# Block mask spread by copies, beta2 as an extra column, and a reordered first load in a sparse-attention and ResMLP kernel

## The chip, the cores and the metric

The kernel runs on one core of a Trainium2 chip. The metric is the device time of one execution in microseconds, and the figure quoted is the median of several runs. Engines are named as the profile names them: PE is TensorE's matmul stream and PEld its weight loads, DVE is VectorE, ACT is ScalarE, POOL is GpSimd, and SP is SyncE, which here issues DMAs only.

## The reference, cut to what matters

Two stages follow one another. The first is block-sparse attention over 4 batches of 8 heads, 768 positions, head size 64. A block of 32 keys is visible to a block of 32 queries if it is a neighbour, if either is the first or the last block, or if it is one of three sampled blocks of that query block.

```python
scores = scale * np.matmul(q, k.transpose(0, 1, 3, 2))
...
for qb in range(n_blocks):
    for kb in sampled_blocks[qb]:
        mask[qb * block:(qb + 1) * block, kb * block:(kb + 1) * block] = True
scores = np.where(mask, scores, -1000000000.0)
...
return np.matmul(attn, v).astype(np.float32)
```

The mask is the same for all heads and batches. The second stage takes the attention output, with the heads side by side, as x of 4 x 768 x 512:

```python
a1 = alpha1 * x + beta1
tok = np.einsum('ts,bsd->btd', w_tok, a1)
u = x + lam * tok
a2 = alpha2 * u + beta2
ch = np.maximum(a2 @ w_ch1, 0.0) @ w_ch2
return (u + lam * ch).astype(np.float32)
```

w_ch1 is 512 x 2048 and w_ch2 is 2048 x 512. Because beta2 is added before w_ch1, beta2 @ w_ch1 is a vector of 2048 numbers that is the same for every row. The kernel uses it as the bias of the ReLU.

## The kernel before, in words

**Tiling.** Work goes in 16 head pairs (four to a batch). Each pair has 9 units (lines 1014 to 1094). A unit is the transposed scores of one 128 x 1024 piece: matmuls into a PSUM tile `sps` of 1024 columns (`emit_qk_full`, L906, or `emit_qk_rows`, L925), one exponential on ACT into an fp16 tile `eT` (L935), and eight matmuls of 65 columns each that multiply `eT` by V and a column of ones (L961). Two `sps` tiles exist, and four one-bank tiles `gb` of 512 columns serve everything else. After the fifth and the ninth unit, DVE divides by the sum (L977, L980) and writes `x_sb`.

**Two ways to mask.** For pairs 0 to 4 (T0 = 5) the mask is part of the score matmul: 24 more contraction rows (the slice MB, partitions 64 to 87) hold, on the key side, an indicator of the key's block and, on the query side, 0 or -400. For pairs 5 to 15 the scores are made with 64 rows alone, two heads' halves of the array at a time, and DVE multiplies `eT` by a stored 0/1 mask `msk` of 128 x 2 x 2560 fp16 (L942, 99 times). The stored mask is built once (`mask_ops`, lines 697 to 745): six pairs of matmuls of 24 rows and 384 columns into `sps` (L707), six exponentials of 128 x 768 on ACT (L728), and one DVE copy of its first 256 columns to its end (L742). It is built from the indicator rows of pair 4's tile, and each `mult` depends on it.

**Preparing a pair.** Pairs 0 to 4 are transposed on PE (L418) and copied by DVE or ACT. From pair 5 on, SP issues DMA transposes of q (L812, two of them) and k (L835), and then two DMAs (`swap`, L855) that copy the first 384 query columns of one partition half to the other half, so that both row halves of the array have what they read. The matmuls of such a pair wait for all of these.

**The ResMLP.** After a pair, DVE makes `a1p` (L1130, L1141), PE mixes tokens (L1179), DVE adds (L1203) and scales to bf16 `ub` (L1217). `ub` is transposed to `uT`: by PE for batch 0, by SP's DMA transposes (L1289) for the others. When four pairs are done, the channel mixer runs in two halves of 384 rows for each batch. Each half has 16 groups of four matmuls of 384 columns into a `gb` bank (`ch1`, L1321), each followed by a ReLU with bias on DVE (L1351) or ACT (L1343), and then twelve groups of four matmuls of 512 columns (`ch2`, L1383). DVE adds the result (L1405) and SP stores it. The half numbered kk = 0 is the first of batch 0.

**The bias.** DVE casts beta2 to `be2b` (L652). Four groups of 16 one-column matmuls (L662) multiply it with w_ch1, and four DVE copies (L673) move four columns at a time to `b1t`, which the ReLUs read.

**The start.** SP issues `sampi` (the sampled blocks, L350), then the two halves of pair 0's q (L352, L354), then three small indicator loads (L356). ACT's queue issues pair 0's k (L351, L353). DVE makes a 24 x 24 block table `mbb` from `sampi` (L400, L406). PE multiplies it (L423), and DVE (L435) and ACT (L432) turn that into the mask rows. PE transposes the first k and then q (L418 by way of `transposes`), ACT and DVE copy them (L447), and the first score matmul follows. `keep_warm` matmuls (L385) fill gaps. In program order DVE's L400 and L406 stand ahead of the cast of q (L413), and PE's L423 stands ahead of both transposes.

**What sets the order.** All later work is given to a planner (`Plan`, lines 102 to 264). Every operation has a cost, a due time and dependencies; the planner simulates the engines, picks the ready operation that is due first, and thereby writes each engine's program order, which is then pinned. An operation offered to both DVE and ACT (`both`) goes to whichever is free first. Loads, DMA transposes and other DMAs have assumed durations (`queued`, `beside`). A list SEEDS shifts due times of early operations by random amounts. Costs and due times thus decide order only; they are not times of the chip.

Of the kernel before, what the change touches and what calls it, by code (L numbers as in the profile page):

```python
# [24 lines left out]
S = 768  # L25
# [21 lines left out]
T0 = 5  # L47
FINE = 3
SEEDS = [2000008, 2000011, 2000019, 2000022, 2000031, 2000062, 2000071, 2000092, 2000133, 2000145, 2000148, 2000158, 2000173, 2000177, 2000195, 2000260, 2000269, 2000429, 2000572, 2000889, 2001074, 2001979, 2002135]
# [52 lines left out]
class Plan:  # L102
# [3 lines left out]
    def __init__(self, pools, free):  # L106
        self.pools = {k: list(range(n)) for k, n in pools.items()}
        self.free = dict(free)
        self.ops = []
        self.users = {}  # L110
        self.slot = {}
        self.held = {}
        self.reader = {}
        self.shifted = False
        self.exps = 0
        self.dma = 6500.0
        self.ring = []
        self.occ = None
        self.loads = []
        self.hw = 0.0  # L120
        self.segs = []
# [146 lines left out]
def kernel(  # L268
# [51 lines left out]
    be2b = pp.tile([P, 4], BF, name="be2b", tag="be2b")  # L320
# [13 lines left out]
    uT = many(3, [P, 4, S], BF, "uT")  # L334
# [14 lines left out]
    k2f = wk.tile([P, 2, NT * D], FP, name="k2f", tag="hts", bufs=2)  # L349
    nc.sync.dma_start(sampi[MB, :], sampled_blocks.bitcast(I32))  # L350
    nc.scalar.dma_start(k2f[:, 0, :], pair_ap(k, 0, 0)[:, 0, :])  # L351
    nc.sync.dma_start(q2f[:, 0, :], pair_ap(q, 0, 0)[:, 0, :])  # L352
# [96 lines left out]
    for t in vext:  # L449
# [5 lines left out]
        dict(PE=5600, ACT=5600, DVE=5750, POOL=3700, SP=4000),  # L455
# [8 lines left out]
    def sl(key):  # L464
        return pl.slot[key][1]
# [91 lines left out]
    def bc_load(nm, t, src, due):  # L557
        def emit(op):
            nc.gpsimd.dma_start(t[:], src.unsqueeze(0).to_broadcast([P, DM]))

        BC[nm] = load(("bc", nm), 640, due, emit)
# [23 lines left out]
    LD[("v", 0)] = landed(("v", 0), 7200)  # L585
# [36 lines left out]
    for g in range(4):  # L622
# [29 lines left out]
        lambda op: nc.vector.tensor_copy(out=be2b[:], in_=be2T[:]),  # L652
# [3 lines left out]
    for g in range(4):  # L656
        key = ("mmb", g)

        def e_mm(op, g=g, key=key):
            for f in range(4):  # L660
                for dk in range(4):
                    nc.tensor.matmul(  # L662
                        bank(key)[:, f : f + 1],
                        w1b[:, dk, ts(4 * g + f, P)],
                        be2b[:, dk : dk + 1],
                        start=(dk == 0),
                        stop=(dk == 3),
                    )

        mm = pl.pe(("be2m", g), 420, 37 + 2.5 * g, e_mm, deps=[W1[g], be2c], need=[(key, GB)])  # L670

        def e_b(op, g=g, key=key):
            nc.vector.tensor_copy(out=b1t[:, ts(g, 4)], in_=bank(key)[:, 0:4])  # L673

        B1T.append(pl.dve(("b1t", g), 165, 36.5 + g, e_b, deps=[mm], uses=[key]))
# [20 lines left out]

    def mask_ops():
        for g in range(3):
            for r in range(2):
                key = ("sps", "m", g, r)  # L700
                due = 9 * T0 - 10 + 2 * g + r

                def e_mm(op, g=g, r=r, key=key):
                    i = sl(("qk", T0 - 1))
                    for w in range(2):
                        o = ORD[r][3 * w]
                        nc.tensor.matmul(  # L707
                            spsT[sl(key)][:, w * 512 : w * 512 + HS],
                            kx2[i][MB, 0, ts(2 * g + r, P)],
                            qx2[i][MB, 0, :].rearrange("p (o t) -> p o t", o=NT)[  # L710
                                :, o : NT : 2, :
                            ],
                            start=True,
                            stop=True,
                        )

                mm = pl.pe(
                    ("mskm", g, r),
                    520,
                    due,  # L720
                    e_mm,
                    deps=PREP[T0 - 1],
                    need=[(key, [("sps", 0)])],
                    uses=[("qk", T0 - 1)],
                )

                def e_x(op, g=g, r=r, key=key):
                    nc.scalar.activation(  # L728
                        msk[:, r, g * S : (g + 1) * S].rearrange("p (w c) -> p w c", w=2),
                        spsT[sl(key)][:].rearrange("p (w c) -> p w c", w=2)[:, :, 0:HS],  # L730
                        AF.Exp,
                        bias=0.0,
                        scale=SCALE,
                    )

                MASK.append(pl.act(("mskx", g, r), act(768), due, e_x, deps=[mm], uses=[key]))
        MASK.append(
            pl.dve(
                ("mskc",),
                dve(512, 4),  # L740
                9 * T0 - 3,
                lambda op: nc.vector.tensor_copy(out=msk[:, :, HF:MW], in_=msk[:, :, 0:256]),  # L742
                deps=MASK[0:2],
            )
        )
# [60 lines left out]
    def prep_rows(pi):  # L806
# [3 lines left out]
        def e_q(op, h):  # L810
# [5 lines left out]
            [("SP", 1250, beside(480, 1250))],  # L816
# [8 lines left out]
            [("SP", 1250, beside(480, 1250))],  # L825
# [7 lines left out]
        def e_k(op):  # L833
# [8 lines left out]
            [("SP", 1250, beside(960, 1250))],  # L842
# [7 lines left out]
        for r in range(2):  # L850

            def e_s(op, r=r):
                i = sl(key)
                lo, hi = slice(r * D, (r + 1) * D), slice((1 - r) * D, (2 - r) * D)
                nc.sync.dma_start(qx2[i][lo, :, HS:S], qx2[i][hi, :, 0:HS])  # L855

            res.append(
                pl.add(
                    ("swap", pi, r),
                    [("SP", 450, beside(380, 450, 40))],  # L860
                    9 * pi - 100,
                    e_s,
                    deps=[t0, t1],
                    uses=[key],
                )
            )
# [3 lines left out]
    for i in range(2):  # L870
# [5 lines left out]
            deps=[landed(("f", i), 5400 - 300 * i)],  # L876
# [140 lines left out]
    while i < NI:  # L1017
# [22 lines left out]
        occ = 437 if pi < T0 else 640  # L1040
# [11 lines left out]
        for j, key in zip(batch, keys):  # L1052
# [23 lines left out]
            for a in unit_heads(uj):  # L1076
# [5 lines left out]
                    30,  # L1082
# [13 lines left out]
    for pi in range(NP):  # L1096
# [188 lines left out]
        else:  # L1285
            for v2 in range(2):

                def e_ud(op, uk=uk, b=b, n=n - 1 + v2, v2=v2):
# [8 lines left out]
                        [("SP", 1250, beside(960, 1250))],  # L1297
# [10 lines left out]
        for hf in range(2):  # L1308
# [5 lines left out]
            for f in range(16):  # L1314
                bk = ("mmh", kk, f)

                def e_c1(op, b=b, hf=hf, f=f, bk=bk, hk=hk):
                    if f == 0:
                        htsT[hk] = wk.tile([P, 16, HS], BF, name="hts", tag="hts", bufs=2)
                    for dk in range(4):  # L1320
                        nc.tensor.matmul(  # L1321
                            bank(bk)[:, 0:HS],
                            w1b[:, dk, ts(f, P)],
                            uT[b % 3][:, dk, ts(hf, HS)],
# [9 lines left out]
                    deps=uts + [W1[f // 4]],  # L1334
# [6 lines left out]
                def e_r(op, f=f, bk=bk, hk=hk):  # L1341
                    if op.eng == "ACT":
                        nc.scalar.activation(  # L1343
                            htsT[hk][:, f, :],
                            bank(bk)[:, 0:HS],
# [4 lines left out]
                    else:  # L1350
                        nc.vector.tensor_scalar(  # L1351
                            out=htsT[hk][:, f, :],
                            in0=bank(bk)[:, 0:HS],
# [13 lines left out]
                        deps=[c1, B1T[f // 4]],  # L1367
                        uses=[bk, hk],
                    )
# [68 lines left out]
    for seed in SEEDS:  # L1438
        r = random.Random(seed)
        part, step = r.choice([0.01, 0.03, 0.1, 0.3]), r.choice([0.5, 1.5, 4])  # L1440
        for op, due in zip(pl.ops, [op.due for op in pl.ops]):
            if r.random() < part and op.due0 < 80:
                op.due = due + r.gauss(0, step)
# [32 lines left out]
```

## Time and profile before

| what | value |
|---|---|
| median of 7 runs | 311.77 us (311.1 to 313.52) |
| the profiled execution's own time | 312.08 us |
| its span in the profile | 310.3 us |
| PE, DVE, ACT, POOL busy | 98%, 74%, 59%, 14% of the span |
| first score matmul (L906) starts | 6.79 us |
| last mask exponential (L728) starts | 58.6 us |
| first multiplication by the mask (L942) starts | 66.8 us |
| first and last ch1 matmul seen in the chain of work | 56.25 and 292.48 us |

Busy time is the union of the instructions' durations. A matmul's duration includes the time that it takes to drain, while the next one is already streaming, so the distance between two starts (the pitch below) says how much of PE a matmul uses. The difference of 1.8 us between the profiled execution's time and its span lies outside of the instructions.

### The profile page before, as it was taken

The numbers are of one execution on the slowest core, as the hardware profiler recorded it, in microseconds if no ns is written. First come the engines' busy times: TensorE is split into PE (matmuls) and PEld (weight loads), VectorE is DVE, ScalarE is ACT, GpSimd is POOL, SyncE is SP. The second block draws the span as 40 slices with busy tenths as digits, with TensorE's granted clock in tenths as the row PEclk, the third lists the DMA queues.
The fourth block names the chain that finished last, engine by engine and source line by source line (L and its number), as shares of the span: only waits on it lengthen the run. The fifth ranks groups of instructions, "written<-read, shape, count | busy, mean of one in ns | idle before, by whom it ended". The sixth has DMA issues, their size and how long they took to land.

```text
span 310.3 us, 7223 instructions
## 1 busy us (share of the span) xinstructions
PE 304.4 (98%) x3023; PEld 183.3 (59%) x3023; DVE 228.8 (74%) x417; ACT 182.5 (59%) x223; POOL 44.7 (14%) x71
## 2 busy tenths in 40 slices
PE   7999999999999999999999999999999999999995
PEld 3687887565475565555665565555655665555543
DVE  6769789987799787777887688768976575555531
ACT  4999898988667754786577755968677310000000
POOL 8465522322101001111000000000000000000000
PEclk9999999999999999999999999999999999999999
DMA  7999999999779484773533334304030122001011
GB/s 153 203 250 195 205 177 190 204 181 170 111 93 150 84 122 59 171 111 60 105 77 73 86 60 78 87 33 81 11 76 34 36 49 72 34 34 36 35 67 68
DMA packets 52592, 31.97 MB, mean 103 GB/s; under 512 B 29448, under 2 KB 48976, under 8 KB 52560
## 3 DMA queue, kind: packets, MB, share of 16 engines
q0 software_dynamic: 17520, 15.47, 33.5%
q1 hardware_dynamic: 34752, 15.65, 23.4%
q8 instruction: 23, 0.38, 0.5%
q10 hardware_dynamic: 288, 0.39, 0.4%
q14 instruction: 9, 0.07, 0.1%
HBM read 30.78 MB, written 6.29 MB: 119 GB/s over the span
## 4 chain that ended last, share of the span: by engine, by line
PE 91%; ACT 2%; DMA 2%; DVE 2%; issue 1%; SPq 0%; ACTq 0%
PE gb L1321 27%; PE gb L1383 26%; PE gb L961 12%; PE gb L1179 10%; PE sps L925 8%; PE sps L906 5%; ACT eT L935 2%; PE gb L418 2%; DMA uT<-ub 1%; DMA q2f<-in_q_dram 1%; PE sps L707 1%; PE gb L662 0%; DVE eT L942 0%; PE gb L385 0%; DVE ot L1405 0%
## 5 line engine op out<-in xcount | busy, mean ns | idle before, releaser
L935 ACT ACTIVATE eT<-sps 128x1024 f16<-128x1024 f32 x144 | 139.5, 1024 | 42.2 <-PE sps L925 35.4
L1321 PE MATMUL gb<-uT,w1b 128*128 128x384 bf16 x512 | 98.7, 326 | 0.2 <-DMA uT<-ub 0.2
L1383 PE MATMUL gb<-w2b,hts 128*128 128x512 bf16 (+2 forms) x400 | 95.2, 370 | 0.0
L942 DVE TENSOR_TENSOR eT<-eT,msk 128x1024 f16<-128x1024 f16 x99 | 66.2, 685 | 10.2 <-ACT eT L935 10.0
L1321 PEld LDWEIGHTS <-w1b 128*128 128x128 bf16 x512 | 46.4, 97 | 32.5 <-issue 2.0
L961 PEld LDWEIGHTS <-eT 128*128 128x128 f16 x1152 | 49.1, 97 | 25.0 <-DVE eT L942 4.7
L1351 DVE TENSOR_SCALAR hts<-gb,b1t 128x384 bf16<-128x384 f32 x64 | 39.4, 617 | 30.5 <-PE gb L1321 30.2
L961 PE MATMUL gb<-vext,eT 128*128 128x65 f16 x1152 | 56.8, 193 | 0.6 <-DVE vext L999 0.6
L1383 PEld LDWEIGHTS <-hts 128*128 128x128 bf16 x400 | 36.1, 97 | 34.5 <-issue 2.1
L1343 ACT ACTIVATE hts<-gb,b1t 128x384 bf16<-128x384 f32 x64 | 36.7, 583 | 24.8 <-PE gb L1321 22.4
L1179 PE MATMUL gb<-a1p,wtokT 128*128 128x256 bf16 (+1 forms) x360 | 35.5, 251 | 0.0
L1179 PEld LDWEIGHTS <-wtokT 128*128 128x128 bf16 x360 | 29.0, 98 | 4.9 <-issue 1.6
L925 PE MATMUL sps<-qk 64*128 64x256 bf16 (+1 forms) x264 | 30.1, 326 | 0.0
L906 PE MATMUL sps<-qk 88*128 88x512 bf16 (+1 forms) x120 | 27.4, 334 | 0.2
L1405 DVE TENSOR_TENSOR ot<-x_sb,gb 128x512 f32<-128x512 f32 (+2 forms) x25 | 16.6, 664 | 10.3 <-PE gb L1383 10.1
L1203 DVE TENSOR_TENSOR x_sb<-x_sb,gb 128x512 f32<-128x512 f32 (+1 forms) x26 | 16.6, 642 | 5.7 <-PE gb L1179 5.5
L980 DVE TENSOR_TENSOR x_sb<-gb,rcp 128x384 f32<-128x384 f32 x32 | 17.8, 558 | 1.1
L925 PEld LDWEIGHTS <-qk 64*128 64x128 bf16 x264 | 8.9, 94 | 16.4 <-issue 13.6
L542 POOL DMA_DIRECT2D q<-in_q_dram x15 | 10.6, 704 | 48.0 <-DMA qk<-q 39.4
L1217 DVE TENSOR_TENSOR ub<-x_sb,a_bc 128x512 bf16<-128x512 f32 (+1 forms) x26 | 16.5, 646 | 0.5
L1141 DVE TENSOR_TENSOR a1p<-a1p,b_bc 128x768 bf16<-128x768 bf16 (+1 forms) x17 | 15.4, 905 | 0.1
L1130 DVE TENSOR_TENSOR a1p<-x_sb,a_bc 128x768 bf16<-128x768 f32 (+1 forms) x17 | 15.4, 905 | 0.1
(69 smaller groups left out, 131.8 us busy)
## 6 DMA issues: line engine op xcount, KB each, us to landing
out_dram<-ot SPq DMA_DIRECT2D x23, 256.0 KB, 2.2
v<-in_v_dram POOLq DMA_DIRECT2D x16, 192.0 KB, 9.0
k<-in_k_dram POOLq DMA_DIRECT2D x15, 192.0 KB, 8.0
q<-in_q_dram POOLq DMA_DIRECT2D x15, 192.0 KB, 8.9
qk<-qk SPq DMA_DIRECT2D x22, 96.0 KB, 3.6
w1b<-in_moe_w_ch_dram POOLq DMA_DIRECT2D x4, 512.0 KB, 11.9
w2b<-in_moe_w_ch_dram POOLq DMA_DIRECT2D x4, 512.0 KB, 17.6
wtk<-in_moe_w_tok_dram POOLq DMA_DIRECT2D x3, 384.0 KB, 8.6
```

What stands on the lines that cost most here:

```text
L906: nc.tensor.matmul(spsT[sl(key)][:, o : o + w], kx2[i][0:KC, a, ts(jt, P)], qx2[i][0:KC, a, c : c + w], start=True, stop=True,)
L925: nc.tensor.matmul(spsT[sl(key)][:, o : o + w], kd[i][rows, h, g, :], qx2[i][rows, h, c : c + w], start=True, stop=True,)
L935: nc.scalar.activation(eTt[sl(("eT", i))][:], spsT[sl(key)][:], AF.Exp, bias=EXPB, scale=SCALE)
L942: nc.vector.tensor_tensor(out=e, in0=e, in1=msk[:, :, x : x + 512], op=ALU.mult)
L961: nc.tensor.matmul(bk[:, t * VW : t * VW + D + 1], eTt[sl(("eT", i))][:, ts(col, P)], vx[:, a, jt, 0 : D + 1], start=(r == 0), stop=(r >= ...
L980: nc.vector.tensor_tensor(out=x_sb[:, s0 : s0 + NT, h * D : (h + 1) * D], in0=o[:, :, 0:D], in1=rc[:].unsqueeze(2).broadcast_to([P, NT, D] ...
L1179: nc.tensor.matmul(bank(bk)[:, j * wp * P : (j + 1) * wp * P], wtokT[:, s, ts(m * g + j, P)], a1p[sl(ak)][:, s, 0:wp, :].rearrange("p w c ...
L1203: nc.vector.tensor_tensor(out=s, in0=s, in1=tp, op=ALU.add)
L1321: nc.tensor.matmul(bank(bk)[:, 0:HS], w1b[:, dk, ts(f, P)], uT[b % 3][:, dk, ts(hf, HS)], start=(dk == 0), stop=(dk == 3),)
L1343: nc.scalar.activation(htsT[hk][:, f, :], bank(bk)[:, 0:HS], AF.Relu, bias=b1t[:, f : f + 1], scale=1.0,)
L1351: nc.vector.tensor_scalar(out=htsT[hk][:, f, :], in0=bank(bk)[:, 0:HS], scalar1=b1t[:, f : f + 1], scalar2=0.0, op0=ALU.add, op1=ALU.max,)
L1383: nc.tensor.matmul(bank(ck)[:, cs], htsT[hk][:, nk, ts(mt, P)], w2h["t"][:, nk, cs], start=(nk == 0), stop=(nk == 15),)
```

## The change

- **Mask.** The six pairs of 384-column matmuls become twelve matmuls of 24 columns (two for each of the six key tiles), into one `gb` bank. They read 24 query columns (`some`: three in each 16 of the first 128), one for each query block. One exponential of 288 columns writes `few`. Nine DVE copies then spread each value over the 5 or 6 columns that share a query block, with an input of step 0 in the innermost dimension. The copy L742 now waits for all nine.
- **beta2.** `be2T` is cast into column 15 of a `uT` tile of the first batch that is 16 columns wider. In the half kk = 0, and there alone, the ch1 matmuls read 385 columns from column 15, so column 0 of each bank holds the bias of that group. A DVE copy for each of the 16 groups moves it to `b1t`, and the ReLU of that group waits for it and reads the bank from column 1. The 64 one-column matmuls and their four copies are gone.
- **Start.** SP issues the first half of q ahead of `sampi`.
- **Swap.** Pair 5's two swaps are DVE copies; those of pairs 6 to 15 stay DMAs.
- **Planner.** Assumed costs, due times, start times and the list of seeds differ, so the order of the work differs in many places.

```diff
-SEEDS = [2000008, 2000011, 2000019, ...]
+SEEDS = [1000001, 1000004, 1000170, ...]
...
-        self.dma = 6500.0
+        self.dma = 6900.0
...
+    uT = [
+        pp.tile([P, 4, S + (0 if i else 16)], BF, name=f"uT{i}", tag=f"uT{i}") for i in range(3)
+    ]
+    be2u = uT[0]
+    uT[0] = be2u[:, :, 16 : S + 16]
...
+    nc.sync.dma_start(q2f[:, 0, :], pair_ap(q, 0, 0)[:, 0, :])
+    nc.scalar.dma_start(k2f[:, 0, :], pair_ap(k, 0, 0)[:, 0, :])
     nc.sync.dma_start(sampi[MB, :], sampled_blocks.bitcast(I32))
-    nc.scalar.dma_start(k2f[:, 0, :], pair_ap(k, 0, 0)[:, 0, :])
-    nc.sync.dma_start(q2f[:, 0, :], pair_ap(q, 0, 0)[:, 0, :])
...
-        dict(PE=5600, ACT=5600, DVE=5750, POOL=3700, SP=4000),
+        dict(PE=5700, ACT=5700, DVE=5750, POOL=4000, SP=4000),
...
-        lambda op: nc.vector.tensor_copy(out=be2b[:], in_=be2T[:]),
+        lambda op: nc.vector.tensor_copy(out=be2u[:, :, 15], in_=be2T[:]),
...
+    RUNS = [[0, 6, 11, 16], [0, 5, 11, 16], [0, 5, 10, 16]]
+
     def mask_ops():
...
+            some = qx2[i][MB, 0, 0:P].rearrange("p (a x) -> p a x", x=16)[:, :, 1:12:5]
+            for n in range(12):
+                r, g = divmod(n // 2, 3)
+                nc.tensor.matmul(
+                    bank(key)[:, ts(n, NBLK)],
+                    kx2[i][MB, 0, ts(2 * g + r, P)],
+                    some,
+                    start=True,
+                    stop=True,
+                )
...
+            nc.scalar.activation(
+                few, bank(key)[:, 0 : 12 * NBLK], AF.Exp, bias=0.0, scale=SCALE
+            )
...
+        for n in range(9):
+            m, c = divmod(n, 3)
+            i0, i1 = RUNS[m][c : c + 2]
...
+                out_ = msk[:, :, 0:HF].rearrange("p r (w x) -> p r w x", x=HS)[:, :, :, ts(m, P)]
+                nc.vector.tensor_copy(
+                    out=out_.rearrange("p r w (a i) -> p r w a i", i=16)[:, :, :, :, i0:i1],
+                    in_=few[:, :, :, :, c : c + 1].broadcast_to([P, 2, 6, 8, i1 - i0]),
+                )
...
-            [("SP", 1250, beside(480, 1250))],
+            [("SP", 1250, beside(1000, 1250, 30))],
...
-                nc.sync.dma_start(qx2[i][lo, :, HS:S], qx2[i][hi, :, 0:HS])
+                move = nc.sync.dma_start if op.eng == "SP" else nc.vector.tensor_copy
+                move(out=qx2[i][lo, :, HS:S], in_=qx2[i][hi, :, 0:HS])
...
+            if pi < 6:
+                o = pl.dve(
...
-        occ = 437 if pi < T0 else 640
+        occ = 437 if pi < T0 else 585
...
-                    30,
+                    31.6,
...
+                w0 = 1 if kk == 0 else 0
+                rhs = [uT[b % 3][:, dk, ts(hf, HS)] for dk in range(4)]
+                if w0:
+                    rhs = [be2u[:, dk, 15 : HS + 16] for dk in range(4)]
...
-                            bank(bk)[:, 0:HS],
+                            bank(bk)[:, 0 : HS + w0],
...
+                        nc.vector.tensor_copy(out=b1t[:, f : f + 1], in_=bank(bk)[:, 0:1])
...
-                            bank(bk)[:, 0:HS],
+                            bank(bk)[:, w0 : HS + w0],
...
-                        deps=[c1, B1T[f // 4]],
+                        deps=[c1, B1T[f]],
```

## The prediction

> **What bounds the kernel now.** I read the page first: the busy shares and the chain that ended last.
>
> ```profile
> PE 304.4 (98%) x3023; PEld 183.3 (59%) x3023; DVE 228.8 (74%) x417; ACT 182.5 (59%) x223; POOL 44.7 (14%) x71
> ...
> PE 91%; ACT 2%; DMA 2%; DVE 2%; issue 1%; SPq 0%; ACTq 0%
> ```
>
> PE is busy for 98% and the chain is PE for 91%. Busy is not proof, since a matmul's duration contains its drain. So I took the starts of all matmuls from the timeline and subtracted what each form needs when it streams (pitches seen: 0.162 us for 384 columns, 0.216 for 512, 0.109 for 256, 0.056 for 128, 0.030 for 65, 0.025 for 1, and about 0.095 more at each change between 128 or 88 array rows and the 64 or 24 rows of L925 and L707). What is left over is PE standing still: 5.1 us in the first 10 us, 1.9 us from 10 to 40, 0.4 us from 40 to 80, 2.2 us from 80 to the end. So after the first 10 us the kernel is a PE stream with under 5 us of holes, and a microsecond of PE work taken out is a microsecond of time, as long as the other engines keep feeding it.
>
> Do they? The table by stage, for the stretches in which the removed work lies:
>
> ```profile
> 40.00:60.00 20.00, 19.99 (x300) 14.56 (x298) 17.99 (x41) 17.56 (x22) 6.10 (x9) 1.00 1.28 189
> 60.00:80.00 20.00, 20.00 (x209) 11.66 (x207) 15.65 (x29) 16.91 (x21) 4.92 (x7) 1.00 1.23 166
> ```
>
> After the length come PE, PEld, DVE, ACT and POOL busy, then the granted clock. From 40 to 60 us DVE (17.99) and ACT (17.56) are nearly full too. That is where the change could fail.
>
> Then the groups, shapes kept apart, for what is removed and for what prices the additions (busy us, mean ns):
>
> ```profile
> L707 PE MATMUL sps<-qk 24*128 24x384 bf16 x12 | 3.0, 326 | 0.0
> L662 PE MATMUL gb<-be2b,w1b 128*128 128x1 bf16 x64 | 2.2, 163 | 0.0
> L728 ACT ACTIVATE msk<-sps 128x768 f16<-128x768 f32 x6 | 4.7, 812 | 0.7 <-PE sps L707 0.7
> L673 DVE COPY b1t<-gb 128x4 f32<-128x4 f32 x4 | 0.6, 154 | 0.0
> L999 DVE COPY vext<-v 128x768 f16<-128x768 f16 x16 | 6.1, 384 | 0.1
> L883 DVE COPY qk<-qk 24x768 bf16<-24x768 bf16 x3 | 1.1, 404 | 0.0
> L688 DVE TENSOR_TENSOR w2b<-w2b,lam_bcb 128x1024 bf16<-128x1024 bf16 x8 | 5.2, 682 | 0.0
> ```
>
> And the PE timeline, for what those matmuls really take from PE:
>
> ```profile
> 38.80 0.54 PE L662 MATMUL gb<-be2b,w1b 128*128 128x1 bf16 x16
> 39.20 0.59 PE L906 MATMUL sps<-qk 88*128 88x512 bf16 x3
> ...
> 51.58 0.28 PE L961 MATMUL gb<-vext,eT 128*128 128x65 f16 x4
> 51.80 0.49 PE L707 MATMUL sps<-qk 24*128 24x384 bf16 x2
> 52.23 1.01 PE L1179 MATMUL gb<-a1p,wtokT 128*128 128x128 bf16 x15
> ```
>
> Sixteen one-column matmuls hold PE for 39.20 - 38.80 = 0.40 us. A mask pair holds it from 51.70 (the four L961 take 4 x 0.030) to 52.23, so 0.53 us: two streams of 0.162, and some 0.2 us of changing rows on the way in and out.
>
> **The change part by part.** PE first.
> - Mask matmuls removed: 6 x 0.53 = -3.15 us.
> - Mask matmuls added: twelve in one run. One change in and out is 0.19 us. Each pitch is at least L662's 0.025, at most L707's weight load of 0.092 not hidden. L707's second matmul starts only 0.012 later than its columns demand, so weights of 24 rows load beside the stream: I take 0.04, near the lower end. 0.19 + 12 x 0.04 = +0.65 us (0.5 to 1.3).
> - beta2 matmuls removed: 4 x 0.40 = -1.6 us.
> - The 385th column: 64 matmuls x 1/2.4 ns = +0.03 us. The read starts at an odd element. L961 reads V at steps of 66 elements and takes an odd 65 columns at full pitch, but its starts are even, so an odd start is not shown; at half rate it would cost 64 x 0.162 = +10.4 us, and a gain has no reason. I take +0.03, being nearest to L961.
>
> PE's sum is -4.1 us, all of it after 10 us.
>
> ACT: six exponentials go (-4.9 us by 6 x 0.812) and one of 288 columns comes, about 0.4 us on the line through L728 and a 384-column ReLU (0.583): -4.5 us, from 52 to 59 us, where ACT is full. It is not the bound, so I count nothing but room.
>
> DVE: nine spreading copies of 96 x 5 or 6, 512 elements in the mean. By the row (L999: 768 in 384 ns, four a cycle above some 0.18) they take about 0.31 each, 2.8 us in all. Against it stands the Trainium skill, "VectorE: DVE Perf Modes", section "What auto-detection actually checks": packing two 16-bit values needs every tensor at a step of one, which an input of step 0 is not; the two read ports alone remain, so two elements a cycle. That is 512/2/0.96 + 0.15 = 0.42 each, 3.8 us; at one a cycle 0.69, 6.2 us. L999 has unit steps, so the rule decides the value: 3.8, range 2.8 to 6.2. The bias copies: 16 x 0.154 instead of 4 x 0.154, +1.85 us, most in 56 to 75. Two swaps at L883's 0.40: +0.8. Together +6.45 us.
>
> What covers it: 40 to 60 held 17.99; with mask 3.8, swaps 0.8, three bias copies 0.5 and without L673's 0.6 it is 22.5 in 20, so 2.5 us must go later. It can: L688 (8 x 0.68 = 5.4 us, from 52.7 to 62.8) is needed by ch2 only at 75.4. Then 60 to 80 holds 15.65 + 2.5 + 2.0 = 20.1, again too full by itself, but ACT has 40 - 34.5 + 4.5 = 10 us free there and takes ReLUs at 0.58 each. Without that cover PE would wait for the 2.5 us. I take 0.5 us of new PE holes (0 to 2.5).
>
> New waits. A kk = 0 ReLU waits for a DVE copy: some 0.25 us later, and its bank with it; behind it on ACT stand exponentials, and PE needs the bank. Sixteen times, hidden while attention fills PE (PE has 0.4 us of holes there now); counted in the 0.5. The swaps wait on DVE for q's transposes, issued at 36.05 and landed 8.2 us later; behind them stand DVE's norms and casts, for which PE waits. Now SP issues them at 46.4, after the landing, and they land 6.9 us later; k's transpose lands at 51.8 anyway and the first matmul with pair 5 comes at 64, so a swap from 46 to 60 is free. Zero (0 to 2 if placed too early; no gain, since PE is full). SP loses two DMAs of 0.6 us; behind them nothing waits. The mask itself is ready at 59.4 now and first used at 66.8, so 7 us of slack take the longer path of PE, ACT and nine copies.
>
> The start:
>
> ```profile
> 0.74 0.44 SPq L350 DMA_DIRECT2D sampi<-in_sampled_blocks_dram  x1
> 1.25 0.37 SPq L352 DMA_DIRECT2D q2f<-in_q_dram  x1
> ...
> 2.56 0.22 DVE L400 TENSOR_TENSOR eqt<-sampi,wtokT 24x72 bf16<-24x72 int32 x1
> ...
> 3.44 0.11 PEld L423 LDWEIGHTS <-mbb 24*24 24x24 bf16 x2 [0.84 <-DVE identb L392]
> ...
> 4.85 0.52 DVE L413 CAST relp<-q2f 128x384 bf16<-128x384 f32 x1 [1.57 <-DMA q2f<-in_q_dram]
> 4.93 0.97 ACT L447 COPY qk<-gb 64x384 bf16<-64x384 bf16 x2 [0.17 <-PE gb L418]
> ```
>
> DVE waits 1.57 us for q, which is the first thing in the chain of work. Issued at 0.74 beside k, whose first half took 2.4 us, and itself 3.6 before, q should land between 3.1 and 4.3 instead of 4.83. But `sampi` now goes second, and L400, L406 and L423 stand ahead of q's cast on DVE and of the transposes on PE. By the row, a 576-byte load issued 0.5 us later is there by 3.05 (2.56 + 0.5): L423 follows at 3.9, ACT's copy of k at 5.4, the first score matmul at about 6.4, a gain of 0.35. By the rule of the skill ("DMA: Bandwidth & Descriptors", section "Queues, rings and completion order": each engine takes one queue's descriptors in ring order) `sampi` lands behind the 192 KB of q, between 3.4 and 4.4. L400 at X puts L423 at X + 0.88, ACT's copy at X + 2.37 to X + 3.34, the first score matmul at X + 3.43: 6.8 to 7.8 instead of 6.79. I believe the order of the ring, take X = 3.7, and get 7.1: +0.3 us, all of it PE standing still (range -0.4 to +1.0).
>
> The reordering by other seeds and costs can fill at most the 4.5 us of holes that are left after 10 us, and can open others; I take zero, plus or minus 1.
>
> Sum: -4.1 + 0.5 + 0.3 = -3.3 us. Against the profiled execution's own 312.08 (span 310.3 and 1.8 outside) that is 308.8; the median of the runs is 0.3 lower, 311.77, so 308.5.
>
> **Rivals.**
> - *PE's work goes, the cover is thin.* DVE's 2.5 us of overflow lands on PE: -4.1 + 2.5 + 0.3 = -1.3, 310.5 us. For: DVE and ACT at 90% and 88% from 40 to 60. Against: 5.4 us of L688 can be put off.
> - *Slower: DVE becomes the bound between 45 and 65 us.* The nine copies run at one element a cycle (6.2 us), so 40 to 60 would hold 24.9; if the planner does not put L688 behind, 4.9 us of adds, casts and ReLUs come late and PE dries up before ch1 starts: -4.1 + 4.9 + 0.3 = +1.1, 312.9 us. It decides from 3.8 us of new PE holes on (0.4 us there now). For: the broadcast input, and that PE has little other work before ch1. Against: ACT's freed 4.5 us.
> - *It doesn't do what it says:* twelve small matmuls at the top price or the 385 columns slowed by a quarter (+2.6) leave nothing: 311.8 us. For: no odd start is in the trace. Against: L961's full pitch at any step.
>
> **How the numbers follow.** The forecast has 0.64 (308.5, its own range 307.0 to 309.8: the start's and the reordering's bounds), the thin cover 0.18 (310.5, between 309.8 and 311.3), DVE as the bound 0.12, nothing 0.06. About 0.3%, 0.9 us, is what a measurement of this kernel can tell from no change. Faster takes the forecast and 0.14 of the thin cover: 0.78. Same takes the other 0.04 and 0.05 of the last case: 0.09. Slower is 0.13. The range 307.0 to 311.3 leaves out 0.16 above and some 0.04 below.
>
> **What would show it.** L662 is gone, the mask's twelve matmuls hold PE for about 0.65 us, and the 385-column pitch is 0.163 us. The spreading copies show 0.42 us each. The first score matmul starts near 7.1, with L400 near 3.7. From 40 to 80 PE's holes are under 1 us. The first ch1 matmul comes 2 to 4 us before 56.2, and the last stretch, from the last L1179 on, is as long as now. I am wrong if PE shows waits for DVE between 45 and 65, if 385 columns take clearly over 0.163, or if a later stretch (120 to 130, where a transpose of `ub` is in the chain) opens new holes.

## The result and the profile after

| | before | after |
|---|---|---|
| median of the runs | 312.10 us (31 runs, 310.67 to 314.44) | 309.17 us (12 runs, 308.88 to 310.73) |
| the profiled execution's own time | 312.08 us | 308.99 us |
| its span | 310.3 us | 307.2 us |
| last matmul starts | 306.99 us | 303.79 us |

The ratio is 0.9904, with an interval of 0.9884 to 0.9925: 3.0 us faster (2.3 to 3.6). The forecast was 308.5 against a before of 311.77, so 3.3 us.

In the code after, L707 of before is L691, L728 is L705, L742 is L730, L855 is L844, L688 is L671, L906 is L904, L925 is L923, L961 is L959, L935 is L933, L1179 is L1177, L1321 is L1324, L1383 is L1404, L400 is L403, L413 is L416, L423 is L426. New are L717 (the spreading copies) and L1347 (a group's bias).

From the page: busy time of each engine, and the chain's shares.

```profile
PE 300.7 (98%) x2959; PEld 182.6 (59%) x2959; DVE 231.7 (75%) x436; ACT 180.4 (59%) x222; POOL 44.7 (15%) x71
...
PE 90%; ACT 5%; DVE 2%; issue 1%; DMA 1%; SPq 0%; ACTq 0%
```

PE has 64 instructions and 3.7 us less, which is more than the span lost. PE is still the chain, but ACT's share has grown from 2% to 5%: that is the first hint that another engine has come into the path.

The table by stage (length, then PE, PEld, DVE, ACT, POOL busy, granted clock, DMA share, GB/s):

```profile
40.00:60.00 20.00, 19.75 (x302) 15.54 (x301) 18.86 (x46) 17.95 (x22) 7.13 (x10) 1.00 1.33 190
60.00:80.00 20.00, 20.00 (x178) 11.02 (x177) 17.74 (x43) 16.71 (x24) 4.21 (x6) 1.00 0.97 150
```

Between 40 and 60 us PE was busy for 19.99 us and is now for 19.75. DVE rose to 18.86 there, and to 17.74 from 60 to 80.

The new groups, shapes kept apart (busy us, mean ns of one, idle before):

```profile
L1324 PE MATMUL gb<-uT,w1b 128*128 128x385 bf16 x64 | 11.4, 328 | 0.0
L717 DVE COPY msk<-warm 128x480 f16<-128x480 f16 x6 | 2.5, 464 | 0.0
L1347 DVE COPY b1t<-gb 128x1 f32<-128x1 f32 x16 | 2.2, 151 | 0.1
L717 DVE COPY msk<-warm 128x576 f16<-128x576 f16 x3 | 1.5, 511 | 0.0
```

And the PE timeline around the mask's matmuls:

```profile
45.08 0.29 PE L959 MATMUL gb<-vext,eT 128*128 128x65 f16 x4
45.30 0.55 PE L691 MATMUL gb<-qk 24*128 24x24 bf16 x12
45.78 0.42 PE L959 MATMUL gb<-vext,eT 128*128 128x65 f16 x8
```

The four L959 hold PE until 45.20 (45.08 + 4 x 0.030); the next begin at 45.78. So the twelve mask matmuls cost PE 0.58 us, changes of rows included.

**Where the time went.** I took PE's holes from the starts of all matmuls in the way of the prediction, for both traces:

| stretch, us | before | after | difference |
|---|---|---|---|
| 0 to 20 | 5.55 | 6.20 | +0.65 |
| 20 to 40 | 1.48 | 1.07 | -0.41 |
| 40 to 60 | 0.23 | 1.46 | +1.23 |
| 60 to 80 | 0.20 | 0.22 | +0.02 |
| 80 to the end | 2.21 | 1.67 | -0.54 |
| all | 9.67 | 10.62 | +0.95 |

The last matmul starts 3.2 us earlier and the holes are 0.95 longer, so PE's own work has shrunk by about 4.1 us. The work went as forecast; a quarter of it came back as holes, in the start and from 40 to 60 us. In the first 20 us the count also holds matmuls that run at half the clock (experiment 1). Full clock comes at 9.3 us in the trace of before and at 9.1 in the trace after, so the clock does not make the difference between these two executions.

### The profile page after: what moved, and what is told of

Its sections match the earlier page's. It is cut to its first block, busy times and chain, and to the rows that moved or that the text cites. A ratio compares the mean times of both kernels' runs of the same rounds, so it can differ in the third digit from the quotient of the medians.

```text
span 307.2 us, 7111 instructions
## 1 busy us (share of the span) xinstructions
PE 300.7 (98%) x2959; PEld 182.6 (59%) x2959; DVE 231.7 (75%) x436; ACT 180.4 (59%) x222; POOL 44.7 (15%) x71
## 4 chain that ended last, share of the span: by engine, by line
PE 90%; ACT 5%; DVE 2%; issue 1%; DMA 1%; SPq 0%; ACTq 0%
PE gb L1324 27%; PE gb L1404 27%; PE gb L959 11%; PE gb L1177 10%; PE sps L923 9%; ACT eT L933 4%; PE sps L904 4%; PE gb L421 1%; DMA sampi<-in_sampled_blocks_dram 1%; DVE qk L476 1%; ACT qk L474 0%; PE gb L388 0%; DVE x_sb L978 0%; DVE a1p L1128 0%; DVE ub L1215 0%
## 5 line engine op out<-in xcount | busy, mean ns | idle before, releaser
L933 ACT ACTIVATE eT<-sps 128x1024 f16<-128x1024 f32 x144 | 139.4, 1024 | 43.0 <-PE sps L923 36.9
L1324 PE MATMUL gb<-uT,w1b 128*128 128x384 bf16 (+1 forms) x512 | 96.0, 326 | 0.0
L1404 PE MATMUL gb<-w2b,hts 128*128 128x512 bf16 (+2 forms) x400 | 93.9, 370 | 0.0
L1324 PEld LDWEIGHTS <-w1b 128*128 128x128 bf16 x512 | 47.3, 98 | 35.1 <-issue 3.1
L959 PEld LDWEIGHTS <-eT 128*128 128x128 f16 x1152 | 48.1, 97 | 20.7 <-issue 4.8
L1404 PEld LDWEIGHTS <-hts 128*128 128x128 bf16 x400 | 36.0, 98 | 35.7 <-issue 2.6
L959 PE MATMUL gb<-vext,eT 128*128 128x65 f16 x1152 | 55.4, 193 | 0.4 <-DVE vext L997 0.2
L1371 DVE TENSOR_SCALAR hts<-gb,b1t 128x384 bf16<-128x384 f32 x61 | 37.5, 617 | 23.4 <-PE gb L1324 22.9
L1363 ACT ACTIVATE hts<-gb,b1t 128x384 bf16<-128x384 f32 x67 | 38.4, 583 | 22.5 <-PE gb L1324 19.4
L1177 PE MATMUL gb<-a1p,wtokT 128*128 128x256 bf16 (+1 forms) x360 | 35.0, 251 | 0.0
L1177 PEld LDWEIGHTS <-wtokT 128*128 128x128 bf16 x360 | 29.3, 98 | 4.7 <-issue 0.8
L923 PE MATMUL sps<-qk 64*128 64x256 bf16 (+1 forms) x264 | 30.1, 326 | 0.0
L904 PE MATMUL sps<-qk 88*128 88x512 bf16 (+1 forms) x120 | 27.2, 334 | 0.6 <-ACT eT L933 0.3
L923 PEld LDWEIGHTS <-qk 64*128 64x128 bf16 x264 | 8.9, 94 | 14.6 <-issue 11.5
L545 POOL DMA_DIRECT2D v<-in_v_dram x15 | 10.6, 704 | 39.9 <-DVE vext L997 31.2
```

The lines of the kernel that those rows point to most:

```text
L545: nc.gpsimd.dma_start(ld[w][sl(key)][:], pair_ap(src, b, n))
L904: nc.tensor.matmul(spsT[sl(key)][:, o : o + w], kx2[i][0:KC, a, ts(jt, P)], qx2[i][0:KC, a, c : c + w], start=True, stop=True,)
L923: nc.tensor.matmul(spsT[sl(key)][:, o : o + w], kd[i][rows, h, g, :], qx2[i][rows, h, c : c + w], start=True, stop=True,)
L933: nc.scalar.activation(eTt[sl(("eT", i))][:], spsT[sl(key)][:], AF.Exp, bias=EXPB, scale=SCALE)
L959: nc.tensor.matmul(bk[:, t * VW : t * VW + D + 1], eTt[sl(("eT", i))][:, ts(col, P)], vx[:, a, jt, 0 : D + 1], start=(r == 0), stop=(r >= ...
L1177: nc.tensor.matmul(bank(bk)[:, j * wp * P : (j + 1) * wp * P], wtokT[:, s, ts(m * g + j, P)], a1p[sl(ak)][:, s, 0:wp, :].rearrange("p w c ...
```

## The experiments

The theory after the result: PE's work sets the time; the q-first start gives some of the gain back, and DVE's copies make the holes from 40 to 60. The rivals: the start is neutral, the holes come from ACT or from the order, and the removed PE work was never all on the path. Each kernel is run beside the kernel before (median 311.73 for the first four; 311.85 for the others, which ran on another chip). The traces of the experiments lack some 30 matmul records each, so I compare starts in them, not sums of holes.

**1. The change with `sampi` issued first again.**

```diff
+    nc.sync.dma_start(sampi[MB, :], sampled_blocks.bitcast(I32))
+    nc.scalar.dma_start(k2f[:, 0, :], pair_ap(k, 0, 0)[:, 0, :])
     nc.sync.dma_start(q2f[:, 0, :], pair_ap(q, 0, 0)[:, 0, :])
-    nc.scalar.dma_start(k2f[:, 0, :], pair_ap(k, 0, 0)[:, 0, :])
-    nc.sync.dma_start(sampi[MB, :], sampled_blocks.bitcast(I32))
```

> The changed kernel with the sampled blocks issued ahead of q on SP again, everything else the same, the planned order included. Theory (one queue's loads land in the order of issue, and the block table stands ahead of the cast of q on DVE and of the transposes on PE): the sampled blocks are read before 2.6 us instead of 3.99, the first score matmul comes at about 6.8 instead of 7.18, and since PE is the bound from then on the whole 0.4 us is won: 308.8 us against 309.17. Rival (ACT's exponentials or the PE clock absorb the start): the first score matmul moves, the time stays at 309.2.

Measured: 307.24 us (307.12 to 308.26), ratio 0.9863 [0.9840, 0.9887]. It is the fastest kernel of this study; against the change as given it is 0.9863/0.9904 = 0.996, with both intervals combined 0.993 to 0.999. The start after the change, from its timeline (start us, duration, engine, line):

```profile
0.74 0.40 SPq L353 DMA_DIRECT2D q2f<-in_q_dram  x1
1.21 0.44 SPq L355 DMA_DIRECT2D sampi<-in_sampled_blocks_dram  x1
...
3.99 0.23 DVE L403 TENSOR_TENSOR eqt<-sampi,wtokT 24x72 bf16<-24x72 int32 x1 [1.35 <-DMA sampi<-in_sampled_blocks_dram]
...
7.18 1.91 PE L904 MATMUL sps<-qk 88*128 88x512 bf16 x5
```

and with `sampi` first:

```profile
2.72 0.23 DVE L403 TENSOR_TENSOR eqt<-sampi,wtokT 24x72 bf16<-24x72 int32 x1
...
4.15 0.51 DVE L416 CAST relp<-q2f 128x384 bf16<-128x384 f32 x1 [0.69 <-DMA q2f<-in_q_dram]
...
6.04 1.03 PE L904 MATMUL sps<-qk 88*128 88x512 bf16 x5 [0.34 <-DVE qk L450]
```

`sampi`, issued 0.47 us later behind q on the same queue, is read 1.27 us later, and the first score matmul starts 1.13 us later. The two L904 rows show a second thing: the same five matmuls take 1.91 us in one and 1.03 in the other. The row of the granted clock prints full speed for both, but the pitch does not: here TensorE still ran at half its clock. By the pitches (128-column transposes 0.107 against 0.056) full speed came at 9.1 us in the one and at 5.0 us in the other. With it, the first exponential is 1.60 us later in the change as given, and the last matmul 1.86 us; from 14 us to the end the lag of each exponential stays between 1.75 and 1.89. Nothing of the start's delay is absorbed later.

**2. The kernel before with q first.**

```diff
+    nc.sync.dma_start(q2f[:, 0, :], pair_ap(q, 0, 0)[:, 0, :])
+    nc.scalar.dma_start(k2f[:, 0, :], pair_ap(k, 0, 0)[:, 0, :])
     nc.sync.dma_start(sampi[MB, :], sampled_blocks.bitcast(I32))
-    nc.scalar.dma_start(k2f[:, 0, :], pair_ap(k, 0, 0)[:, 0, :])
-    nc.sync.dma_start(q2f[:, 0, :], pair_ap(q, 0, 0)[:, 0, :])
```

> The kernel before with only the order of the first loads changed: q ahead of the sampled blocks; the planned order is the same. Theory: the first score matmul moves from 6.79 to 7.2 and the time from 312.1 to 312.5. Rival (the earlier q is what counts, as it was first in the chain of work): 311.6. Rival (absorbed): 312.1.

Measured: 312.79 us (311.64 to 313.68), ratio 1.0031 [1.0010, 1.0052]. So the order of the start costs 1.0 us (0.3 to 1.6) in the kernel before too. Its first score matmul is at 7.06 and full clock at 14.5 us. Its exponentials are some 1.94 us behind those of before from 14 us on; 0.43 of that is absorbed after 120 us, where the trace of before has two stalls.

**3. Three quarters of beta2's one-column matmuls left out of the kernel before** (so three quarters of the bias product are not computed).

```diff
-                for dk in range(4):
+                for dk in range(1):
...
-                        start=(dk == 0),
-                        stop=(dk == 3),
+                        start=True,
+                        stop=True,
```

> The kernel before with one of four of the one-column beta2 matmuls in each group (16 of 64; three quarters of the product are left out of the bias), in the same planned order. Theory (PE is a stream without holes from 38 us on, so what is taken out of it is time): 48 x 0.025 = 1.2 us less, 310.9 us. Rival (PE waits for ACT or DVE there, and the work only filled a hole): 312.1.

Measured: 311.40 us (309.77 to 312.15), ratio 0.9988 [0.9972, 1.0004]. Of 1.2 us of PE work that was taken out, 0.4 is seen, and the interval reaches from 0.9 down to nothing. The trace, exponential by exponential beside that of before, shows where it went. It is 1.22 us ahead before the first of the removed matmuls, most of it from its start (first score matmul at 6.07 instead of 6.79, full clock at 7.8 instead of 9.3). Behind the last of them it is 1.50 ahead, and from 60 us on 1.23 again. So hardly anything of the 1.2 us is won in this trace. ACT's and PE's timelines at the first group of beta2's matmuls:

```profile
36.84 5.76 ACT L935 ACTIVATE eT<-sps 128x1024 f16<-128x1024 f32 x6 [0.18 <-ACT eT L935]
```

```profile
37.33 0.41 PE L961 MATMUL gb<-vext,eT 128*128 128x65 f16 x8
37.58 0.24 PE L662 MATMUL gb<-be2b,w1b 128*128 128x1 bf16 x4
37.91 0.59 PE L906 MATMUL sps<-qk 88*128 88x512 bf16 x3
```

Six exponentials run back to back. The four matmuls that are left have streamed by 37.68 (37.58 + 4 x 0.025), but the score matmul starts at 37.91: 0.23 us pass unused. In the kernel before the sixteen filled this time without a gap (38.80 to 39.20). So beta2's work stood in part where ACT's exponentials set the pace, and there it cost little: the rival explains this better than my theory. That these gaps wait for ACT is read from the back-to-back row, as in the change (experiment 6); the profile names no releaser.

The lead from the start is then lost at one place, on SP's queue and on PE:

```profile
68.67 1.25 SPq L855 DMA_DIRECT2D qk<-qk  x2
```

```profile
76.09 0.39 PE L925 MATMUL sps<-qk 64*128 64x512 bf16 x2
77.41 0.39 PE L925 MATMUL sps<-qk 64*128 64x512 bf16 x2 [0.93 <-issue]
```

Between two halves of a row of L925 PE stands for 0.93 us, and the lead falls from 1.23 to 0.12 us (0.65 at the end, since the two stalls of before after 120 us are not in this trace). PE's weight queue holds a semaphore wait of 1.96 us in front of it, begun at 75.4, while the same wait is 0.44 us in the kernel before. The second half of the row reads pair 6's swapped columns. SP issued the two swaps at 68.7 and 69.3, and with DMA nearly full the first landed 6.4 us later, at 75.1; the landing of the second is not in the trace. So these matmuls come at 77.4 although PE is there earlier (77.1 in the kernel before, by the end of its wait). That the wait is for the second swap is read from the code and these times; the profile names no releaser. After the change the swaps are issued from 64.9 on, and the wait lasts 0.05 us.

**4. The change with each of the nine copies issued twice.**

```diff
-                nc.vector.tensor_copy(
-                    out=out_.rearrange("p r w (a i) -> p r w a i", i=16)[:, :, :, :, i0:i1],
-                    in_=few[:, :, :, :, c : c + 1].broadcast_to([P, 2, 6, 8, i1 - i0]),
-                )
+                for _ in range(2):
+                    nc.vector.tensor_copy(
+                        out=out_.rearrange("p r w (a i) -> p r w a i", i=16)[:, :, :, :, i0:i1],
+                        in_=few[:, :, :, :, c : c + 1].broadcast_to([P, 2, 6, 8, i1 - i0]),
+                    )
```

> The changed kernel with each of the nine spreading copies issued twice, in the same planned order: 9 x 0.38 = 3.4 us more DVE work between 47 and 58 us. Theory (DVE has cover, but the copies stand ahead of the adds that lead to the first ch1 matmul, so a part is paid): 0.5 to 1.5 us more, 310.2 us. Rival (DVE is no bound at all there): 309.2. Rival (DVE is the bound, all of it is paid): 312.6.

Measured: 313.45 us (312.86 to 316.85), ratio 1.0073 [1.0046, 1.0100]. For 3.4 us more of DVE (9 x 0.375, six in a row take 2.25) even its fastest run is 3.7 us over the change's median, and the five runs with a mean granted clock of 1.000 lie 3.7 to 4.1 over it, as much as the added DVE work and more. (What the clock of the start added in these runs is not known.) The profiled execution is its slowest, and shows the way from DVE to PE, first in DVE's and then in PE's timeline:

```profile
53.44 5.25 DVE L718 COPY msk<-warm 128x576 f16<-128x576 f16 x12
58.61 0.55 DVE L1202 TENSOR_TENSOR x_sb<-x_sb,gb 128x384 f32<-128x384 f32 x1
59.19 0.56 DVE L1216 TENSOR_TENSOR ub<-x_sb,a_bc 128x384 bf16<-128x384 f32 x1
```

```profile
59.81 0.50 PE L421 MATMUL gb<-identb,ub 128*128 128x128 bf16 x3 [2.95 <-DVE ub L1216]
```

The copies stand in one block ahead of the residual add and of `ub`, for which PE's transposes wait, 2.95 us. And the wait costs once more, by the table of stages of this kernel:

```profile
56.00:60.00 4.00, 1.05 (x13) 0.74 (x12) 3.86 (x10) 1.94 (x2) 0.00 (x0) 0.85 1.34 178
60.00:64.00 4.00, 4.00 (x44) 3.05 (x43) 3.49 (x10) 1.33 (x2) 2.11 (x3) 0.50 1.31 199
```

From 58.8, still in the hole, to 65.6 the granted clock is 0.50. DVE has no cover here: more copies are on the path at once. The change itself shows how closely they fit:

```profile
50.90 2.25 DVE L717 COPY msk<-warm 128x576 f16<-128x576 f16 x6
53.19 0.56 DVE L1201 TENSOR_TENSOR x_sb<-x_sb,gb 128x384 f32<-128x384 f32 x1
```

Its six copies end at 53.15 us, and the add that follows them starts at 53.19, as PE's token mixing ends (53.16).

**5. The copies held back behind batch 0's last uT copy,** in the kernel of experiment 1.

```diff
+    for op in MASK[2:9]:
+        op.after.append(UTD[3][-1])
```

> The changed kernel with the sampled blocks first on SP (as in the first experiment) and seven of the nine spreading copies held back in the plan until the last copy of batch 0's uT; the order of other work shifts with it. Theory (the copies delay the adds that lead to the first ch1 matmul, so that PE finds too little work from 43 to 52 us): PE's holes from 40 to 60 fall from about 1.4 us to about 0.5, 306.3 us against 307.24 of the first experiment. Rival (those holes come from ACT's exponentials and the serial chain of pair 3, the copies only fill gaps of DVE): 307.2 or, with the order disturbed, up to 308.

Measured: 310.03 us (309.12 to 312.05), ratio 0.9946 [0.9919, 0.9973]: slower than experiment 1, where my theory wanted a gain. In its trace seven of the copies run from 55.80 us on, and the order of other work has shifted with them. PE's gaps ahead of the score matmuls are there all the same, at 48.2, 49.1 and 50.0 us, 0.24 us each; the second:

```profile
48.87 0.41 PE L959 MATMUL gb<-vext,eT 128*128 128x65 f16 x8
49.36 0.59 PE L904 MATMUL sps<-qk 88*128 88x512 bf16 x3
```

So these seven copies do not make the gaps; two copies still run ahead of them, from 47.0 us. What makes this kernel slower than experiment 1 is something else: 1.24 us from the start (full clock at 9.5 us instead of 5.0), and 2.0 us in new holes at 58.5, 65.3 and 73.1 us, the longest of which ends with a ReLU of DVE that comes late:

```profile
66.78 0.82 PE L1324 MATMUL gb<-uT,w1b 128*128 128x385 bf16 x4 [1.09 <-DVE hts L1371]
```

The first ch1 matmul comes at 55.41 us against 54.91.

**6. The small exponential issued six times,** planned as 1.75 us more of ACT near 47 us.

```diff
-            nc.scalar.activation(
-                few, bank(key)[:, 0 : 12 * NBLK], AF.Exp, bias=0.0, scale=SCALE
-            )
+            for _ in range(6):
+                nc.scalar.activation(
+                    few, bank(key)[:, 0 : 12 * NBLK], AF.Exp, bias=0.0, scale=SCALE
+                )
```

> The changed kernel with the one small mask exponential issued six times, in the same planned order: 5 x 0.35 = 1.75 us more ACT work at 47 us. Theory (ACT sets the pace there: its exponentials stand back to back from 47 to 52.7 us and PE waits for them, so that ACT's relief is what lets the saved PE work become time): 1.0 to 1.8 us more, 310.6 us against 309.17. Rival (PE is the bound and ACT has room): 309.2.

Measured: 313.09 us (310.84 to 315.25), ratio 1.0039 [1.0008, 1.0071]. In the trace the six take 2.53 us from start to start where one takes 0.33 in the change, so 2.20 us more, and the lag of the exponentials behind the change's grows by just as much there. The two fastest runs, 310.84 and 311.26, are 1.7 and 2.1 us over the change's median: about the added ACT time. They are also the only two with a mean granted clock of 0.999 or more; the other ten have 0.989 to 0.995. The profiled execution (315.15, clock 0.989) shows why:

```profile
50.00:54.00 4.00, 2.12 (x14) 1.15 (x14) 1.99 (x5) 3.70 (x6) 1.19 (x2) 0.72 1.23 202
54.00:58.00 4.00, 4.00 (x36) 3.03 (x35) 3.40 (x9) 3.07 (x3) 0.21 (x1) 0.50 1.28 191
```

```profile
51.88 1.01 PE L905 MATMUL sps<-qk 88*128 88x512 bf16 x2 [2.10 <-ACT eT L934]
```

PE waits 2.10 us for an exponential to empty a bank, and from 51.7 to 58.6 it runs at half its clock. ACT, which I had left out of the path, sets the pace at 47 to 52. The change itself shows it in ACT's row and in PE's rows:

```profile
47.07 5.60 ACT L933 ACTIVATE eT<-sps 128x1024 f16<-128x1024 f32 x6
```

```profile
49.05 0.59 PE L904 MATMUL sps<-qk 88*128 88x256 bf16 x3
49.49 0.41 PE L959 MATMUL gb<-vext,eT 128*128 128x65 f16 x8
49.97 0.59 PE L904 MATMUL sps<-qk 88*128 88x512 bf16 x3
50.40 0.41 PE L959 MATMUL gb<-vext,eT 128*128 128x65 f16 x8
50.89 0.59 PE L904 MATMUL sps<-qk 88*128 88x512 bf16 x2
```

Six exponentials run back to back, one in 0.93 us, and PE's score matmuls start 0.92 us apart although PE needs less: in each round some 0.24 us pass unused ahead of L904 (49.49 + 8 x 0.030 = 49.73, and L904 starts at 49.97). Three such gaps are 0.7 of the 1.46 us of holes from 40 to 60.

**7. The mask's matmuls issued four times,** 36 x 0.033 = 1.2 us more of PE.

```diff
-            for n in range(12):
+            for n in [x for _ in range(4) for x in range(12)]:
```

> The changed kernel with the twelve small mask matmuls issued four times, in the same planned order: 36 x 0.033 = 1.2 us more PE work at 45 us. Theory (before the first ch1 matmul PE has holes, so work there is not paid one for one, as the quarter beta2 experiment suggests): 0 to 0.5 us more, 309.4 us. Rival (PE is a stream without holes, all is paid): 310.4.

Measured: 311.58 us (309.71 to 312.24), ratio 0.9968 [0.9944, 0.9993]. The runs fall into two groups, five from 309.7 to 310.2 and seven from 311.5 to 312.3. The profiled one is of the upper group, with full clock from 14.3 us on instead of 9.1. Beside the trace of the change its exponentials are 1.59 us later from the 7th to the 35th, and 2.74 later from the 36th to the last: a step of 1.15 us at the added work, of which nothing is won back. The lower group lies where these 1.15 us alone would put it (310.1), the upper where both would (311.7). So PE's work near 45 us is paid in full; that the holes behind it would take it up, as I had thought, is wrong. It delays ACT's row of exponentials, and these set the pace.

**8. The change with q first on SP and `sampi` ahead of k on ACT's queue.**

```diff
+    nc.scalar.dma_start(sampi[MB, :], sampled_blocks.bitcast(I32))
     nc.scalar.dma_start(k2f[:, 0, :], pair_ap(k, 0, 0)[:, 0, :])
-    nc.sync.dma_start(sampi[MB, :], sampled_blocks.bitcast(I32))
```

> The changed kernel with q still first on SP, and the sampled blocks first on ACT's queue, ahead of k; the planned order is the same. Theory (the sampled blocks must not stand behind a large load of their own queue; the earlier q alone wins nothing, as ACT's copy of k sets the first score matmul): sampled blocks read near 2.7, first score matmul near 6.1, 307.3 us. Rival (k being 0.4 us later is paid): 307.7. Rival (the early q wins more): 306.8.

Measured: 308.94 us (308.64 to 311.02), ratio 0.9915 [0.9885, 0.9945], no better than the change. `sampi` is read at 2.67 and q at 3.32, but k only at 4.46 instead of 3.70, and ACT's cast of k now leads the chain: first score matmul at 6.71, full clock at 11.6. At the first exponential it is 0.47 us ahead of the change, and level with it by 14 us; full clock comes 2.5 us later. So this order of the loads won nothing, and what it would be worth at the same clock is not shown.

## Why the prediction was right, and where its terms were off

The sum held: -3.3 forecast, -3.1 between the profiled executions. Its largest term, PE's work, held as well; that the smaller ones cancelled is luck in part. Its steps one by one:

| step | forecast, us | measured, us |
|---|---|---|
| PE's work in all | -4.1 | about -4.1 |
| of this, the mask's twelve matmuls | +0.65 | +0.58 |
| of this, the 385th column | +0.03, pitch 0.163 | about +0.1, pitch 0.164 (384: 0.162) |
| a spreading copy | 0.42 | 0.38 from start to start (2.25 / 6) |
| a bias copy; a swap on DVE | 0.154; 0.40 | 0.151; 0.355 |
| the one small exponential | about 0.4 (its line gives 0.53) | 0.42 |
| `sampi` read; first score matmul | 3.7; 7.1 | 3.99; 7.18 |
| holes of the start (0 to 20) | +0.3 | +0.65 |
| holes from 40 to 80 | +0.5 | +1.25 |
| holes from 20 to 40 and after 80 (reordering) | 0 (plus or minus 1) | -0.95 |

**PE's work** was right. The column read from an odd start costs almost nothing, so the rival of nothing gained falls.

**DVE's price** was right by the rule that I chose over the unit-step row. The two widths give the slope: (511 - 464) ns for 96 elements more, 0.49 ns each, so about the two elements a cycle of the prediction's estimate (512/2/0.96), not four and not one. With that the slower rival lost its price of 6.2 us. Its mechanism is real, though: experiment 4 puts 3.4 us on DVE at the same place and lands at 313.45, slower than the kernel before.

**The cover** came as argued for DVE; for ACT it was mis-argued. The eight scalings of L688 (now L671) run from 58.6 to 73.5 us instead of 52.7 to 62.8, and ACT takes 16 of the 22 ReLUs before 80 us instead of 9 of 18; from 60 to 80 PE has only 0.22 us of holes. But those from 40 to 60 came out at 1.46, so from 40 to 80 the holes are not under 1 us, and what they wait for most is not DVE but ACT: attention runs ahead (the 45th exponential starts at 57.10 instead of 63.14, the last score rows of 88 array rows end 6.5 us earlier) and nine exponentials stand in 10.0 us where they stood in 18.0. "It is not the bound, so I count nothing but room" is the sentence that failed: ACT's 4.5 us of room were filled at once, and there ACT set the pace, which experiments 6 and 7 show. In a row of exponentials it did so in the kernel before, too (experiment 3). The thin cover's 310.5 was not reached, but its holes went half the way. For the same reason the first ch1 matmul is not 2 to 4 us earlier but 0.6 later (56.77): PE did attention in the time it had won, and got it back after 60 us. The last stretch kept its length: from the last token-mixing matmul (L1179 before, L1177 after) to the last matmul 56.30 us in both.

**The start** had the right mechanism and too small a price. The order of the ring held, and `sampi` landed behind q. But I measured the loss against one execution of before in which q was late (its cast at 4.85). Others with the same order show 4.15, 4.20 and 4.53, with the first score matmul at 6.04, 6.07 and 6.31; the five traces with q first on SP and `sampi` second lie at 7.03 to 7.23. Against the mean of the four with `sampi` first (6.30) the loss is 0.8 us, not 0.3. The half clock, which I did not consider, adds to it. It also makes the first reading wrong: of the first 10 us, in which I counted 5.1 us of PE standing still, PE is busy for 8.06, and most of the 5.1 are matmuls at half speed. By the runs the new order costs 1.0 us in the kernel before and 1.3 in the change (0.3 to 2.2); the profiled executions of the change and of experiment 1 differ by 1.9.

**"A microsecond of PE work taken out is a microsecond of time"** is not true by itself. Its condition, that the other engines keep feeding PE, does not hold in a row of back-to-back exponentials: experiment 3 took 1.2 us out of before, and hardly any of it was won. Nor does it hold at 77 us, where a wait, most likely for pair 6's swap, took a lead of 1.1 us. In the change that swap is issued 6 us earlier, and the wait is gone. So the planner's part was more than the zero I gave it: it cleared the way at 77. How much of the 0.95 us of holes is its doing is not shown: 0.54 of it is two stalls near 126 and 193 us (0.36 and 0.18) that are gone, and they are gone in experiment 3 too, in the order of before. Two terms too small by about 1.1 in all and one too large by 0.95 cancelled.

What stays open: how the 3.0 us divide between the mask, beta2 and the order alone. Kernels with the mask alone, with beta2 alone, with both in the old order, and with the new order alone were not run. That the order of start decides when full clock comes is not settled either: with `sampi` first it came at 5.0, 7.8, 9.3 and 9.5 us, with `sampi` behind q at 9.1, 14.2, 14.3, 14.5 and 14.5.

## What to carry to other kernels

Where the busiest engine loses work, ask which engine fills the room: here attention ran ahead and ACT, freed of 4.5 us, set the pace for 5 us of it. Before you price a start from one trace, look how far its first landings vary, and keep the small load on which the chain hangs ahead of the large ones in the queue. Undo the parts that were not the point: here the old order of three loads was worth about 1 us on its own. And lay two traces beside each other step by step: a lag that stays constant tells where it arose.

## What the runs showed of the hardware that was not expected

- The clock of the start: matmuls ran at half speed until between 5.0 and 14.5 us, depending on the execution, while the page's clock row printed full speed. Only the pitches show it (512 columns 0.427 against 0.216 us). Experiment 7 has the loads and the order of the change; its first exponential is 0.05 us later, and with full clock at 14.3 us instead of 9.1 it is 1.59 behind from the 7th on, so this alone is worth about 1.6 us. With one trace per kernel it is the likely but not the shown reason for the groups of times in experiments 5 and 7, which lie 1.8 apart in 7, and for the 3.8 us between the runs of before.
- A short hole halves the clock later too. In experiment 6 the clock fell 1.95 us after PE had stopped and in experiment 4 1.96 us after, and it stayed at 0.50 for 6.8 us in both. The Trainium skill, "TensorE: Matmul & The Clock Gate", Part 1, speaks of a free-running activity window of 3.4 us. The traces agree: the clock changes at 14.18, 51.73 and 58.56 us in experiment 6 and at 14.44, 58.82 and 65.64 in experiment 4, which are 11, 2, 13 and 2 times 3.41 us apart. The same part gives the rule to leave no idle gap over about 3.4 us on PE; here a hole of 2.10 us was enough, within a window in which PE worked for less than half (about 1.45 of the last 3.41 us before the clock fell).
- A 24-row matmul of 24 columns has a pitch of 0.033 us, close to the 0.025 of a single column, with its weight loads hidden beside it.
